# Two attention layers and two MLPs on one core: some row transposes move from TensorE to crossbar DMA

## The chip, the cores and the metric

The kernel runs on one core of a Trainium2 chip. The metric is the device time in microseconds (us). The core has TensorE (PE, with its weight loads shown as PEld), VectorE (DVE), ScalarE (ACT), GpSimd (POOL) and SyncE (SP). In this kernel SP issues all data movement by DMA, in the order of its queue: a DMA that waits for its data holds up every DMA behind it on SP. Eight DMA semaphores are used in turn, so a DMA also waits until the one eight places before it has landed.

## The reference

Four layers, each added to its own input: linear attention (A), MLP (B), A, B, on 2048 rows of 576 elements in bf16. Both kinds normalise rows first.

```python
def _layernorm(x, axis=-1, eps=1e-5):
    m = jnp.mean(x, axis=axis, keepdims=True)
    v = jnp.var(x, axis=axis, keepdims=True)
    return (x - m) / jnp.sqrt(v + eps)

# A: 32 heads of 18; phi(t) = where(t > 0, t + 1, exp(t)) + 1e-6
q, k, v = split_heads(x @ wqkv)              # wqkv 576 x 1728
kv  = sum over rows of phi(k) outer v        # per head
z   = sum over rows of phi(k)
o   = (phi(q) @ kv) / (phi(q) @ z + 1e-6)
return o @ wo                                # wo 576 x 576

# B: its own layernorm of an already normalised row; w1 576 x 4608, w2 4608 x 576
return gelu(layernorm(x) @ w1 + b1) @ w2 + b2
```

A and B use the same weights both times.

## The kernel before, in words

Rows are worked on in 16 tiles of 128 (t = 0 to 15). TensorE contracts over the partition axis, so normalised rows must be turned: column tile t of `yT` (128 partitions, KD = 5 blocks of 128 features, 2048 rows) holds the transposed rows of tile t, the last block holding 64 real features. Blocks of four tiles (512 rows, c = 0 to 3) are the unit of queries and of the MLP.

`LNPipe` carries each tile through normalisation. A tile is fed, and each `tick` moves it one stage on: statistics (on DVE by `bn_stats`, or on ACT), reciprocal root on POOL (line 433), a mean product (line 436), the norm itself (DVE for the first tiles of the first layer, POOL from tile 4 on, line 444; POOL for the first block of an MLP, line 466) and then the turning. `hold` leaves a tile alone for so many ticks. The recorded order within an engine is mostly the program's order; some instructions are tied to follow others by scheduling-only dependencies.

Rows are turned in one of two ways. With `evac` "act", PE transposes the five blocks against an identity into one PSUM bank (line 500) and ACT copies the bank into `yT` (line 505). With `evac` "dma", DVE turns 32 x 32 squares and a DMA through DRAM puts them in place; later MLP blocks and the second attention layer use this, and it does not change. The first way serves all 16 tiles of the first layer and, in both MLPs, the four tiles of the first block.

The first layer runs in rounds. For t from 4 to 15 a round is: the keys of tile t in two halves (`k_half`, line 653: five matmuls each, needing column tile t of `yT`), then `pre_a1`, which feeds a later tile, ticks the pipe and issues one piece of the weights that come later (`late_pieces`), then two steps of mask building on POOL, one group of queries (line 621) and the product of rows and keys (line 678). The function phi of a key half is either exp and identity on ACT with two steps on DVE (`phi_from_psum`) or exp on ACT and two steps on DVE of which one reads PSUM (`phi_by_dve`); the half chooses. The statistics of the tile that is fed follow the last phi on DVE.

The DMAs of the first layer's start and of the later weights are tied into one chain on SP (`chained`): input rows, wqkv, then the pieces of w1 (nine, three DMAs each), wo in their midst, then w2 (six pieces of 864 KB) with the bias b2 behind the second, then b1, then the residual rows `xo`.

After the keys come the small products of attention and then `wo_stage` for t from 0 to 15 (line 933): ten matmuls into a PSUM pair, a sum with the residual row on DVE (line 605), and a store of the new row to DRAM (`x_d`, line 612). Its tiles 0 to 3 are fed to the MLP's pipe. The MLP's first matmuls (line 1045) take all four tiles of the first block at once, and use the same PSUM pairs (`hp_ps`) that the sums of the last attention tiles must first have read. SP issues a residual load and a store for every tile there.

Of the kernel before, what the change touches and what calls it, by code (L numbers as in the profile page):

```python
# [15 lines left out]
P = 128  # L16
NT = S // P
KD = 5
# [17 lines left out]
def build(tc, A_x, A_wqkv, A_wo, B_w1, B_b1, B_w2, B_b2, out, dbg=None, n_layers=4):  # L36
    nc = tc.nc
    dbg = dbg or {}
    with ExitStack() as ctx:
# [90 lines left out]
        yT = const.tile([P, KD, S], BF16, name="yT")  # L130
# [4 lines left out]
        NV = 2  # L135
        v_ring = [const.tile([P, G, P], BF16, name=f"v_ring{i}") for i in range(NV)]
        AHEAD = 4
        turned = const.tile([P, D // 32, TPC, 32], BF16, name="turned")
        x_d = dpool.tile([NT, P, D], F32, name="x_d")
        yrow_d = dpool.tile([NCB, 4, TPC, 32, D], BF16, name="yrow_d")  # L140
# [112 lines left out]
        def bias_casts():  # L253
# [1 line left out]
            tc.add_manual_dep(cast.ins, pool_last["norm"], NOSYNC, reason="bias is not urgent")  # L255

        late_pieces = [(lambda i=i: piece_w1(i)) for i in range(4)] + [piece_wo] + \
                      [(lambda i=i: piece_w1(i)) for i in range(4, 9)] + [(lambda i=i: piece_w2(i)) for i in range(6)] + [piece_b1_dma]

        state = dict(wo=0, ycnt=0, vcnt=0, turns=0)  # L260
        pool_last = dict(norm=None)
# [85 lines left out]
        class LNPipe:  # L347
# [11 lines left out]
            def tick(self, transposes=1):  # L359
                land()  # L360
                for it in list(self.items):
                    st = it["stage"]
                    if st == 4 and it["evac"] != "dma":
                        if transposes == 0 or state["wo"] < it["tp_at"]:
                            continue
                        transposes -= 1
# [67 lines left out]
                    elif st == 2 and it["norm"] != "dve":  # L434
# [1 line left out]
                        nc.gpsimd.tensor_scalar(out=nmr[:], in0=it["mv"][:, 0:1], scalar1=1.0 if it["stats"] == "act" else -1.0,  # L436
                                                scalar2=it["rstd"][:, 0:1], op0=ALU.mult, op1=ALU.mult)
                        it["nmr"] = nmr
                    elif st in (2, 3) and it["kind"] == "A" and it["evac"] == "act":
                        xt, t = it["xt"], it["t"]  # L440
                        tail = first_tail(t)[:, 0:64]
                        if it["norm"] == "pool":
# [13 lines left out]
                    elif st in (2, 3):  # L456
                        if sum(other["stage"] == 4 for other in self.items) == NY:
                            continue
                        y = y_ring[state["ycnt"] % NY]
                        state["ycnt"] += 1  # L460
                        xt = it["xt"]
                        if it["norm"] == "act":
                            nc.scalar.activation(out=y[:, 0:D], in_=xt[:, 0:D], func=ACT.Identity,
                                                 scale=it["rstd"][:, 0:1], bias=it["nmr"][:, 0:1])
                        elif it["norm"] == "pool":
                            norm = nc.gpsimd.tensor_scalar(out=y[:, 0:D], in0=xt[:, 0:D], scalar1=it["rstd"][:, 0:1],
                                                           scalar2=it["nmr"][:, 0:1], op0=ALU.mult, op1=ALU.add)
                            pool_last["norm"] = norm.ins.name
                        else:
                            norm = nc.vector.tensor_scalar(out=y[:, 0:D], in0=xt[:, 0:D], scalar1=it["mv"][:, 0:1],  # L470
                                                           scalar2=it["rstd"][:, 0:1], op0=ALU.subtract, op1=ALU.mult)
                            if it["after"] == "phi":
                                tc.add_manual_dep(norm.ins, dve_last["phi"], NOSYNC, reason="keys go on first")
                            dve_last["norm"] = norm.ins.name
                        if it["kind"] == "B" and it["evac"] != "dma":
                            nc.gpsimd.tensor_copy(out=y[:, D:DPAD], in_=y[:, 4 * P:D])
                        if it["kind"] == "A" and it["evac"] == "dma":
                            c, j = divmod(it["t"], TPC)
                            nc.sync.dma_start(out=yrow_d[c, :, j], in_=y[:, 0:D])
                        it["y"] = y  # L480
                        it["stage"] = 4
                        continue
                    elif st == 4:
                        t = it["t"]
                        first_layer = it["kind"] == "A" and it["evac"] == "act"
                        y = it["xt"] if first_layer else it["y"]
                        if it["evac"] == "dma":
                            turn_rows(y, t, it["kind"])
                            self.items.remove(it)
                            continue  # L490
                        tp = ps_h.tile([P, 512], F32, name="tp", tag="h")
                        tp = tp[:, 0:DPAD // 2].bitcast(BF16).rearrange("p (k n) -> p k n", k=KD)
                        first = first_layer and t < 2
                        tp2 = tp
                        if first:
                            tp2 = ps_h.tile([P, 512], F32, name="tp2", tag="h")
                            tp2 = tp2[:, 0:DPAD // 2].bitcast(BF16).rearrange("p (k n) -> p k n", k=KD)
                        for k in range(KD):
                            block = first_tail(t, P) if first_layer and k == 4 else y[:, k * P:(k + 1) * P]
                            pe(nc.tensor.transpose(out=(tp if k < 3 else tp2)[:, k, :], in_=block, identity=ident[:]))  # L500
                        if first:
                            named(f"ca{t}", nc.scalar.copy(out=yT[:, 0:3, t * P:(t + 1) * P], in_=tp[:, 0:3, :]))  # L502
                            named(f"cd{t}", nc.vector.tensor_copy(out=yT[:, 3:KD, t * P:(t + 1) * P], in_=tp2[:, 3:KD, :]))
                        elif it["evac"] == "act":
                            turned_tile = nc.scalar.copy(out=yT[:, :, t * P:(t + 1) * P], in_=tp)
                            act_last["turned"] = turned_tile.ins.name
                            if first_layer and t < 5:
                                named(f"ca{t}", turned_tile)
                            elif act_last["exp"] is not None:
                                tc.add_manual_dep(turned_tile.ins, act_last["exp"], NOSYNC, reason="keys go on first")  # L510
                        else:
                            nc.vector.tensor_copy(out=yT[:, :, t * P:(t + 1) * P], in_=tp)
                        self.items.remove(it)
                        continue
# [100 lines left out]
        def layer_A(li, next_kind, pre_a1=None):  # L615
# [34 lines left out]
            def k_half(t, half, defer=False):  # L650
                kp = ps_h.tile([P, 512], F32, name="k_ps", tag="h")
                for k in range(KD):
                    pe(nc.tensor.matmul(kp[:, 0:HALF], lhsT=yT[:, k, t * P:(t + 1) * P],  # L653
                                        rhs=wqkv_sb[:, k, D + half * HALF: D + (half + 1) * HALF],
                                        start=(k == 0), stop=(k == KD - 1)))
                by_dve = half or li == 0 and t == 2

                def phi():
                    if (half, t // 2) not in self_k["pk"]:
                        self_k["pk"][(half, t // 2)] = blk.tile([P, D], BF16, name="pk", tag="blk")  # L660
                    pk = self_k["pk"][(half, t // 2)][:, (t % 2) * HALF:(t % 2 + 1) * HALF]
                    (phi_by_dve if by_dve else phi_from_psum)(kp[:, 0:HALF], pk, P, HALF,
                                                              tag=f"{t}{half}" if li == 0 and t < 4 else None)
                if defer:
                    return phi
                phi()
# [158 lines left out]
            if li == 0:  # L825
# [42 lines left out]
                    rows_by_keys(t, 0)  # L868
                for _ in range(2):
                    q_proj(*q_left.pop(0))  # L870
                masks(len(mask_steps))
            else:
                for t in range(6, NT - TPC):
# [63 lines left out]
            def wo_stage(t):  # L937
# [1 line left out]
                wp = wo_open[t][1]  # L939
                xn = residual(li, t, wp[:, :, 0:HALF])  # L940
                if xn is not None and next_kind == "B" and t < TPC:
                    lnp.feed(xn, t, "B", "pool", "act", hold=(2, 5, 6, 8)[t] if li > 0 else (2, 8, 8, 10)[t], tp_at=6 + 2 * t if li > 0 else (6, 10, 11, 14)[t],
                             **(dict(after="sum") if t in (0, 3 if li > 0 else 2) else dict(stats="act", after="rden")))

            for t in range(AHEAD if li == 0 else AHEAD + 2):
# [173 lines left out]
        def l0_norm_eng(t):  # L1119
            return "pool" if t > 3 else "dve"  # L1120

        def feed0(t, after=None):
            lnp.feed(x0_tiles.pop(t), t, "A", l0_norm_eng(t), "act", after=after)

        pe_chain.update(on=True, last=None)
        warm_pe(9)
# [7 lines left out]
        warm_pe(2)  # L1134

        def pre_a1_layer0(t):
            if t + 3 < NT:
                feed0(t + 3, after=dve_last["phi"])
            lnp.tick()
            if late_pieces:  # L1140
                late_pieces.pop(0)()
            if t == NT - 1:
                piece_b2_dma()
                while late_pieces:
                    late_pieces.pop(0)()

        lbs = {li: LayerB(li, kinds[li + 1] if li + 1 < n_layers else None)
               for li, kind in enumerate(kinds) if kind == "B"}
# [64 lines left out]
```

## Time and profile before

| what | value |
|---|---|
| median of 3 runs | 760.16 us (760.14 to 760.37) |
| span of the profiled execution, first to last instruction | 758.4 us |
| the runs' median less that span | 1.8 us |
| granted TensorE clock, mean | 1.000 |
| first layer's rounds, t = 4 to 15 | 17.9 to 56.8 us |
| first MLP's first matmul / second MLP's | 101.7 us / 473.6 us |
| first matmul with w2 | 136.8 us |
| PE transposes in all | 120 (24 tiles of five) |

The profile gives no time of its own for the profiled execution beside its span; what lies around the span is read as the difference to the runs. A line of the time order gives the start from the beginning of the span, the length, the engine, the source line, the operation, what it writes and reads, and how many instructions were merged. Matmuls overlap, so what a group adds is read from the start of one group to the start of the next. SP's own lines are issues: their length is the time that SP spent on issuing, and the landing is a separate figure (median of an issue of its line).

### The profile page before, as it was taken

The numbers are of one execution on the slowest core, as the hardware profiler recorded it, in microseconds if no ns is written. First come the engines' busy times: TensorE is split into PE (matmuls) and PEld (weight loads), VectorE is DVE, ScalarE is ACT, GpSimd is POOL, SyncE is SP. The second block draws the span as 40 slices with busy tenths as digits, with TensorE's granted clock in tenths as the row PEclk, the third lists the DMA queues.
The fourth block names the chain that finished last, engine by engine and source line by source line (L and its number), as shares of the span: only waits on it lengthen the run. The fifth ranks groups of instructions, "written<-read, shape, count | busy, mean of one in ns | idle before, by whom it ended". The sixth has DMA issues, their size and how long they took to land.

```text
span 758.4 us, 15817 instructions
## 1 busy us (share of the span) xinstructions
PE 753.2 (99%) x6595; PEld 487.4 (64%) x6595; DVE 272.0 (36%) x685; ACT 328.7 (43%) x733; POOL 116.6 (15%) x196
## 2 busy tenths in 40 slices
PE   9999999999999999999999999999999999999998
PEld 5776754774477457646777777457646754774476
DVE  8876862136033503401367577600230131000000
ACT  6887656205600650263057666660174036205600
POOL 4840231002000301200100005300020020001000
PEclk9999999999999999999999999999999999999999
DMA  8994573026312711320404047530240033011000
GB/s 236 267 313 74 178 262 82 17 64 189 83 39 83 181 51 48 109 69 17 131 24 116 24 136 255 185 82 16 88 115 7 16 127 82 9 33 55 1 9 24
DMA packets 80977, 73.90 MB, mean 97 GB/s; under 512 B 36874, under 2 KB 65546, under 8 KB 80906
## 3 DMA queue, kind: packets, MB, share of 16 engines
q1 hardware_dynamic: 80906, 72.90, 33.0%
q8 instruction: 51, 0.84, 0.5%
q14 instruction: 20, 0.16, 0.1%
HBM read 48.10 MB, written 24.77 MB: 96 GB/s over the span
## 4 chain that ended last, share of the span: by engine, by line
PE 97%; DVE 1%; ACT 0%; issue 0%; DVEq 0%
PE m_ps L1104 36%; PE h_ps L1045 21%; PE hp_ps L1045 16%; PE q_ps L621 6%; PE k_ps L653 5%; PE wo_ps L933 5%; PE k_ps L678 4%; PE m_half L1104 1%; PE tp L500 1%; PE warm_ps L217 1%; PE k_tail L678 1%; PE kv_ps L719 0%; PE den_ps L769 0%; PE rden_ps L810 0%; PE kvwo_half L737 0%
## 5 line engine op out<-in xcount | busy, mean ns | idle before, releaser
L1104 PE MATMUL m_ps<-w_sb,hT 128*128 128x288 bf16 x2232 | 274.8, 286 | 0.0
L1104 PEld LDWEIGHTS <-hT 128*128 128x128 bf16 x2304 | 224.3, 98 | 60.4 <-issue 3.4
L1045 PEld LDWEIGHTS <-w_sb 64*128 64x128 bf16 x2304 | 124.5, 94 | 136.4 <-issue 1.9
L1045 PE MATMUL hp_ps<-yT,w_sb 64*128 64x512 bf16 x1152 | 178.0, 376 | 0.0
L1045 PE MATMUL h_ps<-yT,w_sb 64*128 64x512 bf16 x1152 | 148.0, 376 | 0.0
L1050 ACT COPY relay_sb<-relay_sb 128x1 f32<-128x1 f32 x144 | 28.5, 198 | 260.4 <-PE h_ps L1045 217.6
L1041 ACT ACTIVATE hT<-h_ps,b1T 128x512 bf16<-128x512 f32 x144 | 91.0, 683 | 44.1 <-PE h_ps L1045 44.1
L433 POOL TENSOR_TENSOR ln_rstd<-ln_u,neg_half 128x1 f32<-128x1 f32 x61 | 35.2, 577 | 439.9 <-DVE ln_u L415 218.0
L1041 ACT ACTIVATE hT<-hp_ps,b1T 128x512 bf16<-128x512 f32 x144 | 91.1, 692 | 0.0
L605 DVE TENSOR_TENSOR xbf<-m_ps,xo 128x576 bf16<-128x576 f32 x15 | 11.4, 757 | 213.5 <-PE m_ps L1104 213.5
L605 DVE TENSOR_TENSOR xo<-m_ps,xo 128x576 f32<-128x576 f32 x16 | 12.1, 757 | 172.6 <-PE m_ps L1104 172.6
L588 POOL TENSOR_TENSOR xo<-xo,b_bc 128x576 f32<-128x576 f32 x32 | 40.9, 1283 | 97.3 <-DMA xo<-x_d 58.4
L1045 PE MATMUL h_ps<-yT,w_tail 64*128 64x512 bf16 x144 | 54.1, 376 | 0.0
L1045 PE MATMUL hp_ps<-yT,w_tail 64*128 64x512 bf16 x144 | 54.1, 376 | 0.0
L621 PE MATMUL q_ps<-yT,wqkv_sb 128*126 128x512 bf16 (+1 forms) x200 | 49.3, 379 | 0.1
L653 PE MATMUL k_ps<-wqkv_sb,yT 128*128 128x288 bf16 x320 | 44.6, 286 | 0.2
L933 PE MATMUL wo_ps<-kvwo,pq 126*128 126x288 bf16 (+1 forms) x320 | 43.4, 286 | 0.3
L1045 PEld LDWEIGHTS <-w_tail 64*128 64x128 bf16 x288 | 27.1, 94 | 17.1
L653 PEld LDWEIGHTS <-yT 128*128 128x128 bf16 x320 | 31.0, 98 | 8.9 <-ACT yT L502 0.6
L933 PEld LDWEIGHTS <-pq 126*128 126x128 bf16 (+1 forms) x320 | 30.3, 97 | 9.1 <-issue 0.8
L621 PEld LDWEIGHTS <-wqkv_sb 128*126 128x126 bf16 (+1 forms) x200 | 25.7, 131 | 11.7 <-issue 0.5
L554 ACT ACTIVATE phi_e<-q_ps 126x512 bf16<-126x512 f32 (+1 forms) x40 | 23.9, 597 | 18.4 <-PE q_ps L621 16.8
(138 smaller groups left out, 591.6 us busy)
## 6 DMA issues: line engine op xcount, KB each, us to landing
xo<-x_d SPq DMA_DIRECT2D x48, 288.0 KB, 3.5
x_d<-xo SPq DMA_DIRECT2D x32, 288.0 KB, 2.6
xl<-x_d SPq DMA_DIRECT2D x24, 288.0 KB, 4.2
y_d<-turned SPq DMA_DIRECT2D x40, 144.0 KB, 3.1
w_sb<-in_B_w_dram SPq DMA_DIRECT2D x6, 864.0 KB, 10.4
yT<-y_d SPq DMA_DIRECT2D x10, 512.0 KB, 4.2
w_sb<-in_B_w_dram SPq DMA_DIRECT2D x9, 512.0 KB, 5.9
x_d<-xn SPq DMA_DIRECT2D x16, 288.0 KB, 3.3
```

The lines of the kernel that those rows point to most:

```text
L433: nc.gpsimd.tensor_tensor(out=rstd[:], in0=it["u"][:], in1=neg_half[:], op=ALU.pow)
L554: exp = nc.scalar.activation(out=e_out, in_=ps_ap, func=ACT.Exp)
L588: nc.gpsimd.tensor_tensor(out=xo[:], in0=xo[:], in1=b2_bc[:], op=ALU.add)
L605: total = nc.vector.tensor_tensor(out=xn[:, cols].rearrange("p (h n) -> p h n", h=2), in0=halves, in1=xo[:, cols].rearrange("p (h n) -> p ...
L621: pe(nc.tensor.matmul(qp[0:GR[g], :], lhsT=wqkv_sb[:, k, GO[g]:GO[g] + GR[g]], rhs=yT[:, k, c * CA:(c + 1) * CA], start=(k == 0), stop=(k ...
L653: pe(nc.tensor.matmul(kp[:, 0:HALF], lhsT=yT[:, k, t * P:(t + 1) * P], rhs=wqkv_sb[:, k, D + half * HALF: D + (half + 1) * HALF], start=(k ...
L678: pe(nc.tensor.matmul(dst, lhsT=lhsT, rhs=pk, start=(t == 0), stop=(t == NT - 1)))
L933: pe(nc.tensor.matmul(wp[:, half, 0:HALF], lhsT=pq[(g, c)][0:GR[g], j * P:(j + 1) * P], rhs=kvwo[g][0:GR[g], half * HALF:(half + 1) * HALF ...
L1041: act_last["gelu"] = nc.scalar.activation(out=to, in_=ps, func=ACT.Gelu_apprx_tanh, bias=b1T[:, f:f + 1], scale=1.0).ins.name
L1045: mm = pe(nc.tensor.matmul(dst[n], lhsT=wt, rhs=mv, start=(seen[n] == 0), stop=(seen[n] == 8)))
L1050: relay = nc.scalar.copy(out=relay_sb[:, 1:2], in_=relay_sb[:, 0:1])
L1104: pe(nc.tensor.matmul(acc[half][:, 0:cols.stop - cols.start], lhsT=hT[f][:, j * P:(j + 1) * P], rhs=w2_sb[:, f, cols], start=(f == 0), sto ...
```

## The change

Crossbar DMA transposes, issued by SP straight from SBUF into `yT`, take the place of PE transposes with ACT copies for tiles 7 to 15 of the first layer and for the four tiles of the first block of both MLPs. In the first layer a tile takes two DMAs (its first four blocks from the row tile, the last from the ring that holds the row's last 64 features); in the MLP it takes one.

- The first layer's nine pairs are in the chain of SP, in between the weight pieces: two pieces of w1, tiles 7 and 8, a piece, tile 9, a piece, tile 10, wo, tile 11, and so on to tile 15, then the last piece.
- Statistics are fed four tiles ahead from tile 8 on (round 4 feeds tiles 7 and 8).
- The six pieces of w2 and b2 are issued behind the last round; b1 is issued in the last rounds' place of a piece.
- The keys' second half of tiles 7 to 15 goes through `phi_from_psum`.
- Tile 3 of the first MLP is held 9 ticks for 10; the places after which PE transposed (`tp_at`) fall away.

```diff
+        XB = 7
...
-                      [(lambda i=i: piece_w1(i)) for i in range(4, 9)] + [(lambda i=i: piece_w2(i)) for i in range(6)] + [piece_b1_dma]
+                      [(lambda i=i: piece_w1(i)) for i in range(4, 9)] + [piece_b1_dma]
+        w2_pieces = [(lambda i=i: piece_w2(i)) for i in range(6)]
...
-                    if st == 4 and it["evac"] != "dma":
+                    if st == 4 and it["evac"] not in ("dma", "xbar"):
...
+                        if it["evac"] == "xbar":
+                            if first_layer:
+                                chained(nc.sync.dma_start_transpose(out=yT[:, 0:KD - 1, t * P:(t + 1) * P], in_=y[:, 0:4 * P]))
+                                chained(nc.sync.dma_start_transpose(out=yT[:, KD - 1:KD, t * P:(t + 1) * P], in_=first_tail(t, P)))
+                            else:
+                                nc.sync.dma_start_transpose(out=yT[:, :, t * P:(t + 1) * P], in_=y[:])
+                            self.items.remove(it)
+                            continue
...
-                by_dve = half or li == 0 and t == 2
+                by_dve = half and (li > 0 or t < XB) or li == 0 and t == 2
...
+                piece_b2_dma()
+                for _ in range(6):
+                    w2_pieces.pop(0)()
                 masks(len(mask_steps))
...
-                    lnp.feed(xn, t, "B", "pool", "act", hold=(2, 5, 6, 8)[t] if li > 0 else (2, 8, 8, 10)[t], tp_at=6 + 2 * t if li > 0 else (6, 10, 11, 14)[t],
+                    lnp.feed(xn, t, "B", "pool", "xbar", hold=(2, 5, 6, 8)[t] if li > 0 else (2, 8, 8, 9)[t],
...
-            lnp.feed(x0_tiles.pop(t), t, "A", l0_norm_eng(t), "act", after=after)
+            lnp.feed(x0_tiles.pop(t), t, "A", l0_norm_eng(t), "act" if t < XB else "xbar", after=after)
...
-            if t + 3 < NT:
-                feed0(t + 3, after=dve_last["phi"])
+            for ahead in (3, 4) if t == 4 else (4,):
+                if t + ahead < NT:
+                    feed0(t + ahead, after=dve_last["phi"])
             lnp.tick()
-            if late_pieces:
+            if late_pieces and t < NT - 1:
                 late_pieces.pop(0)()
-            if t == NT - 1:
-                piece_b2_dma()
-                while late_pieces:
-                    late_pieces.pop(0)()
```

More of the change, by code (lines that the diff above doesn't have):

```diff
@@ L438, in tick @@
                         it["nmr"] = nmr
-                    elif st in (2, 3) and it["kind"] == "A" and it["evac"] == "act":
+                    elif st in (2, 3) and it["kind"] == "A" and it["evac"] in ("act", "xbar"):
                         xt, t = it["xt"], it["t"]
@@ L484, in tick @@
                         t = it["t"]
-                        first_layer = it["kind"] == "A" and it["evac"] == "act"
+                        first_layer = it["kind"] == "A" and it["evac"] in ("act", "xbar")
                         y = it["xt"] if first_layer else it["y"]
```

## The prediction

> **What bounds the kernel now.** I read the page's busy times first, then the chain, then the order in time of TensorE (PE), GpSimd (POOL) and SyncE's queue (SP) where the change sits.
>
> ```profile
> span 758.4 us, 15817 instructions
> PE 753.2 (99%) x6595; PEld 487.4 (64%) x6595; DVE 272.0 (36%) x685; ACT 328.7 (43%) x733; POOL 116.6 (15%) x196
> PE 97%; DVE 1%; ACT 0%; issue 0%; DVEq 0%
> PEclk9999999999999999999999999999999999999999
> ```
>
> PE is never short of work and always at full clock. So a matmul taken off PE shortens the span by its time, and a wait of PE lengthens it by its time. Nothing else counts. The span is 758.4 us; the median of the runs, 760.16, has 1.8 us more around it, which I leave unchanged, so the sum is taken from 760.16.
>
> PE in order of time in the first layer; start, length, what:
>
> ```profile
> 24.44 1.39 PE L653 MATMUL k_ps<-wqkv_sb,yT 128*128 128x288 bf16 x10
> 25.66 0.39 PE L500 MATMUL tp<-ident,x 128*128 128x128 bf16 x4
> 25.89 0.22 PE L500 MATMUL tp<-ident,v_ring 128*128 128x128 bf16 x1
> 26.02 1.24 PE L621 MATMUL q_ps<-yT,wqkv_sb 128*72 128x512 bf16 x5
> ...
> 27.70 1.39 PE L653 MATMUL k_ps<-wqkv_sb,yT 128*128 128x288 bf16 x10
> ...
> 53.89 1.39 PE L653 MATMUL k_ps<-wqkv_sb,yT 128*128 128x288 bf16 x10
> 55.11 1.24 PE L621 MATMUL q_ps<-yT,wqkv_sb 128*126 128x512 bf16 x5
> ```
>
> A round is 3.26 us (24.44 to 27.70). Five transposes hold PE from 25.66 to 26.02, 0.36 us; the last round has none. They turn tile 7, whose keys start at 27.70.
>
> POOL normalising tile 7, and SP's issues around it:
>
> ```profile
> 23.31 0.77 POOL L444 TENSOR_SCALAR x<-x,ln_rstd,ln_nmr 128x512 bf16<-128x512 bf16 x1
> 24.06 0.39 POOL L444 TENSOR_SCALAR v_ring<-x,ln_rstd,ln_nmr 128x64 bf16<-128x64 bf16 x1
> ```
> ```profile
> 19.14 0.60 SPq L231 DMA_DIRECT2D w_sb<-in_B_w_dram  x1
> 19.78 1.26 SPq L234 DMA_DIRECT2D w_tail<-in_B_w_dram  x2
> ...
> 24.95 0.63 SPq L226 DMA_DIRECT2D wo_sb<-in_A_wo_dram  x1
> 25.62 0.40 SPq L227 DMA_DIRECT2D wo_sb<-in_A_wo_dram  x1
> ```
>
> Tile 7 is normalised at 24.45, 3.25 us before its keys. Nothing on PE, ACT or POOL keeps SP from running ahead: one piece of the first MLP weight costs it 1.94 us (19.14 to 21.08), wo 1.03.
>
> **What goes.** Layer 1: 9 tiles at 0.355 us, 3.2 us of PE. The two MLP entries: 8 tiles, seven at 0.28 us (100.14 to 100.42) and one at 0.52 (466.40 to 466.92, an idle stretch within it), 2.45 us. Together **5.65 us**, all on the path. Seventeen ACT copies of 0.69 us go too, worth nothing, since PE is the bound.
>
> **What comes in layer 1.** The new key passes take 0.41 us on ACT (for 0.69) and 0.32 on DVE (for 0.46), nine each: both lighter, and between 27 and 55 us DVE is busy 23.5 of 28 us, ACT 22.9. I cost them at nothing; if DVE, the fuller, lost that cover, its 2.6 us a round would still be under PE's new 2.91 (3.26 less 0.355).
>
> Two crossbar DMAs per tile are new, and the trace has no such operation. Two prices are unknown. T, SP's time to issue the pair: the nearest rows are plain issues of 0.33 to 0.65 us (lowest T 0.66), and at the other end the bias load of 4608 two-byte elements at 2.31 us (T up to 2.96 with 0.65 for the tail). L, from an issue to its landing: 1.8 us (output rows) to 4.5 (slowest store of `turned`, median 3.1). I take T = 1.2 and L = 3.1, since that store, short runs out of SBUF, is nearest in kind.
>
> Tile 7 is first. Its keys are due at 27.70 - 0.36 = 27.34. Tile 8's statistics now stand between its own on DVE, two starts of 0.37 us, so its norm ends near 24.8 and 25.15. The second DMA goes at 24.8 + 0.6 = 25.4 and lands at 28.5. PE waits **1.2 us**. The DMA rings are near empty then, for SP now stops at these transposes from 21.1 on; the weight pieces stand behind them in its order.
>
> The tiles after: PE wants tile 15 at 27.34 + 8 x 2.91 = 50.6. SP starts on tile 8 at about 26.9 (its norm follows on POOL, 2.1 us after tile 7's), and has eight pairs, six weight pieces and wo: 26.9 + 8T + 6 x 1.94 + 1.03 = 39.6 + 8T, and the landing 2.5 us later. At T = 1.2 that is 51.7, which the first wait already covers. In that stretch the rings carry 6 x 0.59 + 0.66 + 8 x 0.164 = 5.5 MB in 23.6 us, 233 GB/s, against 289 at full share before (27 to 55 us). So a transpose often stands behind part of a weight piece, 0 to 2.0 us (0.59 MB at 289); I take half, **1.0 us**, paid once because the later tiles are then as late as PE. POOL needs 2.1 us per norm and 0.6 for masks, under 2.91; were it over, each tile would add the excess.
>
> The second MLP weight: its six pieces go out from about 52 instead of 40, and need 5.3 MB / 289 = 18 us, so the first residual rows land near 73, before the first sum at 80.3; its first matmul is at 136.8. The first MLP weight ends near 55, needed from 101.7. The bias vector lands before POOL's next norm at 83.9. All hidden by 7 us or more; a DMA stage 7 us slower than this would begin to cost.
>
> **What comes at the MLP entries.** The first block of the first MLP would start at 101.74 - 1.12 = 100.6. Tile 3's norm ended at 98.77; its square now stands on ACT ahead of a table load of 1.28 us and is held one tick less, so I put it at 97.2, and it lands at 100.3: no wait (1.3 us if the norm stays where it was). The next limit is a PSUM pair that the sum of tile 14 must free:
>
> ```profile
> 471.26 0.76 DVE L605 TENSOR_TENSOR xo<-wo_ps,xo 128x576 f32<-128x576 f32 x1 [0.81 <-PE wo_ps L933]
> 473.40 0.76 DVE L605 TENSOR_TENSOR xo<-wo_ps,xo 128x576 f32<-128x576 f32 x1 [1.39 <-DMA xo<-x_d]
> ```
>
> In the second MLP entry DVE waits for residual rows, whatever PE gains, and ends that sum at 474.16. The pair was wanted at 474.44 and is now wanted 1.1 us earlier: **0.85 us** given back; 0.1 at the first entry (sum ends at 101.61, wanted at 101.5). SP's order also puts the transposes of tiles 2 and 3 ahead of the last residual loads, up to 1.3 us if issuing them is dear; those loads wait for POOL anyway.
>
> **Sum.** -5.65 + 1.2 + 1.0 + 0.95 = -2.5; 760.16 - 2.5 = **757.6 us**.
>
> **Rivals.** *Slower: SP cannot issue fast enough.* With T larger, the wait before tile 15 is 39.6 + 8T + 2.5 - 50.6 = 8T - 8.5, with the 1.0 of the rings 8T - 7.5. The gain left, 5.65 - 0.95 = 4.7, is gone at **T = 1.5**. At T = 2 the time is 764.0, at 2.96 it is 771.6. For it: SP has in-order issue and weight pieces of 1.94 us in a round of 2.91, leaving 0.97. Against it: large plain DMAs of 512 runs cost only 0.4 to 0.6 us to issue. [...]
>
> *Better: wholly hidden.* With L = 1.8 tile 7's tail lands at 27.2, no wait: 760.16 - 4.7 = 755.5, or 754.5 if the residual loads come early too. For it: empty rings at 25 us; against it: only output stores land so fast.
>
> *Much slower: the crossbar holds the rings.* If each pair keeps them for r us, a round is r + 2.0 against 2.91; above r = 0.9 each of eight tiles adds the excess. At r = 4, 25 us of waiting, 780. The one row of element-wise movement, the bias load, took 12.7 us, but behind four pieces of the second weight. [...]
>
> **How the numbers follow.** Forecast (755.5 to 759.5): 0.46. Wholly hidden: 0.10. SP too slow: 0.34, its lower edge reaching 759 and most of it below 768. Rings held: 0.05. The change does nothing, gains given back exactly: 0.05. Taking 0.2% (1.5 us), about what a measurement tells from no change, the forecast gives 0.41 of faster, and hidden 0.10; the rest of the forecast, the 0.05 and the edge of the SP case give same 0.13; slower 0.36. The range 754.8 to 768 leaves out the held rings, the dearest issues, and a little below; the forecast's own range is 755.5 to 759.5.
>
> **What would show it.** PE: 85 transposes fewer; the keys' line then waits for a DMA on `yT`, 1 to 2 us near 27, little after. SP: the new issue lines' lengths give T, the landing L. A wait that comes back at every tile from 9 to 15 means T or the rings; one at 100 or 472 us means tile 3 was late; a DVE wait for residual rows near 473 with PE idle is the 0.85. It is wrong if T exceeds 1.5 us, or if L exceeds about 5.6 us (L - 1.9 for tile 7, plus 1.0, against 4.7).

## The result and the profile after

The changed kernel takes **778.83 us** (777.47 to 780.19) against 760.26 us for the kernel before: 1.0243 times as long, 95% interval 1.0228 to 1.0258. The forecast was 757.6 us, its range ended at 768, and the direction was wrong. The profiled execution has a span of 775.7 us, 17.3 more than before.

From the page of the changed kernel: the span, the busy times, the chain that ended last, and the granted clock.

```profile
span 775.7 us, 15669 instructions
PE 754.3 (97%) x6510; PEld 487.6 (63%) x6510; DVE 268.4 (35%) x685; ACT 321.4 (41%) x725; POOL 116.8 (15%) x196
PE 83%; DMA 2%; DVE 1%; ACT 0%; issue 0%; POOL 0%; SPq 0%; DVEq 0%; POOLq 0%
PEclk9999999999999999999999999999999999999999
```

PE has 85 matmuls fewer and is idle 21.4 us where it was 5.2; DMA has entered the chain. PE's busy time is no smaller although work was taken away, mostly because some of what is left ran at half clock (three windows of 3.41 us, some 1.7 us each), too briefly for the slices of the clock row to show it.

Where the 17.3 us came in, by the starts of the stages in the two traces (us):

| stretch | before | after | difference |
|---|---|---|---|
| start to the end of layer 1's key rounds | 59.06 | 68.49 | +9.43 |
| output products to the first MLP's first matmul | 23.78 | 27.35 | +3.57 |
| the same at the second MLP | 24.41 | 27.36 | +2.95 |
| second MLP's first matmul to PE's last | 281.90 | 283.33 | +1.43 |

The rest is unchanged. PE's waits in layer 1 (20 to 70 us; what waited for what: total, times, longest), and SP in the same stretch (start, length, what):

```profile
PE k_ps L663 <- DMA yT<-x: 4.5, 2, 2.6
PE k_ps L663 <- DMA yT<-v_ring: 2.2, 2, 1.7
PE k_ps L663 <- ACT phi_a L565: 0.5, 1, 0.5
PE k_tail L688 <- DVE pk L572: 0.4, 1, 0.4
```
```profile
45.25 1.23 SPq L495 DMA_TRANSPOSE yT<-x  x1
46.57 1.18 SPq L496 DMA_TRANSPOSE yT<-v_ring  x1
47.80 0.57 SPq L232 DMA_DIRECT2D w_sb<-in_B_w_dram  x1
48.43 1.26 SPq L235 DMA_DIRECT2D w_tail<-in_B_w_dram  x2
49.79 1.23 SPq L495 DMA_TRANSPOSE yT<-x  x1
```

SP hardly rests here: the gaps between these issues are 0.1 us or less, so it waits neither for a row nor for an earlier DMA. A pair of crossbar DMAs takes it 2.4 us of issue and some 2.6 with the gaps; with a weight piece of 1.9 a round of SP is 4.5 us (45.25 to 49.79), where a round of PE's own work is 2.91.

At the second MLP's entry (447 to 492 us), DVE's wait for residual rows before and then after (total, times, longest), and PE's wait for tile 3:

```profile
DVE xo L605 <- DMA xo<-x_d: 1.4, 1, 1.4
```
```profile
DVE xo L615 <- DMA xo<-x_d: 6.9, 4, 2.4
```
```profile
PE h_ps L1058 <- DMA yT<-y_ring: 1.7, 1, 1.7
```

At the first entry, tile 3's transpose on SP and the MLP's first matmul, which needs it:

```profile
110.71 1.29 SPq L498 DMA_TRANSPOSE yT<-y_ring  x1
```
```profile
114.75 1.04 PE L1058 MATMUL h_ps<-yT,w_sb 64*128 64x512 bf16 x8 [1.32 <-DMA yT<-y_ring]
```

### The profile page after: what moved, and what is told of

Its sections match the earlier page's. It is cut to its first block, busy times and chain, and to the rows that moved or that the text cites. A ratio compares the mean times of both kernels' runs of the same rounds, so it can differ in the third digit from the quotient of the medians.

```text
span 775.7 us, 15669 instructions
## 1 busy us (share of the span) xinstructions
PE 754.3 (97%) x6510; PEld 487.6 (63%) x6510; DVE 268.4 (35%) x685; ACT 321.4 (41%) x725; POOL 116.8 (15%) x196
## 4 chain that ended last, share of the span: by engine, by line
PE 83%; DMA 2%; DVE 1%; ACT 0%; issue 0%; POOL 0%; SPq 0%; DVEq 0%; POOLq 0%
PE m_ps L1117 35%; PE h_ps L1058 20%; PE hp_ps L1058 16%; PE q_ps L631 3%; PE k_ps L663 3%; PE k_ps L688 2%; PE wo_ps L946 1%; DMA yT<-y_ring 1%; PE m_half L1117 1%; DMA xo<-x_d 1%; DMA x_d<-xn 0%; DVE xn L615 0%; ACT turned L824 0%; PE k_tail L688 0%; DVE pq L830 0%
## 5 line engine op out<-in xcount | busy, mean ns | idle before, releaser
L1058 PEld LDWEIGHTS <-w_sb 64*128 64x128 bf16 x2304 | 128.4, 94 | 136.6 <-issue 6.5
L663 PE MATMUL k_ps<-wqkv_sb,yT 128*128 128x288 bf16 x320 | 47.6, 295 | 7.6 <-DMA yT<-x 4.5
L564 ACT ACTIVATE phi_e<-k_ps 128x288 bf16<-128x288 f32 x38 | 15.6, 410 | 48.3 <-PE k_ps L663 45.8
```

The lines of the kernel that those rows point to most:

```text
L564: exp = nc.scalar.activation(out=e_out, in_=ps_ap, func=ACT.Exp)
L1058: mm = pe(nc.tensor.matmul(dst[n], lhsT=wt, rhs=mv, start=(seen[n] == 0), stop=(seen[n] == 8)))
```

## The experiments

Theory: each crossbar DMA costs SP a fixed 1.2 us of issue, so in layer 1 the queue is the bound, and at the MLP entries the loads of residual rows stand behind the transposes. Rivals: the crossbar or the DMA rings are slow; the later second weight is itself the cause.

### The two halves of the change

Layer 1 alone: the feed at the MLP entries goes back.

```diff
-                    lnp.feed(xn, t, "B", "pool", "xbar", hold=(2, 5, 6, 8)[t] if li > 0 else (2, 8, 8, 9)[t],
+                    lnp.feed(xn, t, "B", "pool", "act", hold=(2, 5, 6, 8)[t] if li > 0 else (2, 8, 8, 10)[t], tp_at=6 + 2 * t if li > 0 else (6, 10, 11, 14)[t],
```

> The change in layer 1 and the later second weight are kept; the two MLP entries turn their rows on TensorE again. Theory 'SP's issue': each crossbar DMA holds SP's queue for about 1.2 us whatever its size, two of them and a weight piece make a round of 4.3 us against PE's 2.9, so layer 1 keeps its whole loss: it ends 9.4 us later than before, two clock halvings in it. The second MLP's entry goes back to 24.4 us (from 27.4), without its halving; the first MLP's entry keeps what the late second weight costs, 1 to 3 us. Sum 760.3 + 9.4 + 1 to 3 = 770.5 to 772.5. Rival 'the entries are only late because layer 1 is': the entries stay as in the changed kernel, 777.

769.82 us (1.0134, interval 1.012 to 1.0148), just under the range. Layer 1 ends 8.60 us late, and the first entry takes 24.88 us (+1.10). The second entry is back at 24.41. The 1.1 us are DVE's wait for the first residual pair, which the kernel before does not have at that sum:

```profile
DVE xn L615 <- DMA xo_pair<-in_A_x_dram: 1.2, 1, 1.2
```

The expected halvings did not come: after 17 us no matmul of this trace is as long as those at half clock. The changed kernel's key matmuls after its wait of 1.94 us, and here after the same wait:

```profile
45.22 2.54 PE L663 MATMUL k_ps<-wqkv_sb,yT 128*128 128x288 bf16 x10 [1.94 <-DMA yT<-x]
```
```profile
45.09 1.40 PE L663 MATMUL k_ps<-wqkv_sb,yT 128*128 128x288 bf16 x10 [1.94 <-DMA yT<-x]
```

The MLP entries alone: the kernel before with only that feed and its DMA.

```diff
+  if it["evac"] == "xbar":
+      nc.sync.dma_start_transpose(out=yT[:, :, t * P:(t + 1) * P], in_=y[:])
+      self.items.remove(it)
+      continue
```

> The kernel before with the crossbar only at the two MLP entries; layer 1 and the order of the second weight as before. Theory 'SP's issue': at the second entry the loads of residual rows stand behind three transposes of 1.3 us each on SP, so that stage takes 27.4 us instead of 24.4, and the half clock behind its wait adds 1.4: +4.4. At the first entry the residual pairs are early again (the second weight was issued long before), so only tile 3's landing is left, 1.3 us less the 1.1 us of transposes gone: +0.2 to +1. Sum 764.5 to 766. Rival 'the crossbar itself is slow at both entries': the first entry loses its 3.6 us too, 768.

769.0 us (1.0111, interval 1.0092 to 1.0129), above the range. The first entry takes 27.65 us although the second weight was issued early, so the late weight is not what costs there. In medians the halves add up: 9.6 and 8.8 above before, 18.6 together in the changed kernel. SP at the first entry, in the kernel before and then here:

```profile
82.04 1.72 SPq L612 DMA_DIRECT2D x_d<-xn  x2
83.88 0.38 SPq L575 DMA_DIRECT2D xo_pair<-in_A_x_dram  x1
```
```profile
82.49 1.72 SPq L616 DMA_DIRECT2D x_d<-xn  x2
86.55 1.34 SPq L492 DMA_TRANSPOSE yT<-y_ring  x1
88.44 0.41 SPq L579 DMA_DIRECT2D xo_pair<-in_A_x_dram  x1
```

SP stands at the transpose until tile 0 is normalised, from 84.2 to 86.55, and the residual pair behind it goes out 4.6 us later than before (4.1 when counted from the stage's own start, which is 0.45 us later here).

### Is it the number of DMAs, or their bytes?

One DMA per tile: the layer-1-only kernel without the one-block transposes (a memset at the start fills their place with zeros).

```diff
-  chained(nc.sync.dma_start_transpose(out=yT[:, KD - 1:KD, t * P:(t + 1) * P], in_=first_tail(t, P)))
```

> Layer 1 alone, with the four-block transposes of tiles 7 to 15 kept and the nine one-block transposes of their last 64 features left out (those rows of the transposed tile are zero, so the result lacks these features). A fifth of the bytes goes, half of the DMAs. Theory 'SP's issue': the pair's 2.4 us become 1.2, a round is 1.2 + 1.9 = 3.1 us against PE's 2.9; layer 1 ends 0 to 3 us earlier than before, not 9.4 later, that is 9 us or so under the layer-1-only kernel: about 761. Rival 'the crossbar or the rings are slow': four fifths of the movement are left, layer 1 keeps 7 us or more of its loss: 768 to 770.

759.71 us in a single run; layer 1 ends at 58.68, 9.0 us earlier than with two DMAs a tile, although four fifths of the bytes are left.

Three DMAs per tile: the same blocks, the wide one split.

```diff
-  chained(nc.sync.dma_start_transpose(out=yT[:, 0:KD - 1, t * P:(t + 1) * P], in_=y[:, 0:4 * P]))
+  for k in (0, 2):
+      chained(nc.sync.dma_start_transpose(out=yT[:, k:k + 2, t * P:(t + 1) * P], in_=y[:, k * P:(k + 2) * P]))
```

> Layer 1 alone; the four-block transpose of each tile 7 to 15 is split into two of two blocks, so each tile has three crossbar DMAs for the same 5 blocks and bytes. Theory 'a fixed issue per DMA': SP's time per tile goes from 2.4 to 3.55 us and a round with a weight piece from 4.4 to 5.5; seven to eight more rounds' worth of 1.17 us, so layer 1 ends 8 to 9 us later than with two DMAs (67.7 -> 76), and the late queue pushes the second weight's loads onto the residual pairs a little more: 778 to 781, against 769.8 with two and 759.7 with one. Rival 'bytes or blocks through the crossbar set the pace': same blocks, no change, 769 to 771.

781.05 us, also a single run. Layer 1 ends at 79.66, 12.0 us later than with two, more than the 8 to 9 expected: SP's eight rounds, 5.80 us for 4.54, give 10.1 of them, and three halvings of the clock lie in the same stretch. The first entry lost nothing more (24.03 us), against the expectation. SP's rows of the kernel with one, then of the one with three:

```profile
43.24 1.23 SPq L496 DMA_TRANSPOSE yT<-x  x1
44.52 0.58 SPq L233 DMA_DIRECT2D w_sb<-in_B_w_dram  x1
45.15 1.27 SPq L236 DMA_DIRECT2D w_tail<-in_B_w_dram  x2
46.52 1.23 SPq L496 DMA_TRANSPOSE yT<-x  x1
```
```profile
46.21 2.46 SPq L496 DMA_TRANSPOSE yT<-x  x2
48.77 1.18 SPq L497 DMA_TRANSPOSE yT<-v_ring  x1
49.99 0.59 SPq L232 DMA_DIRECT2D w_sb<-in_B_w_dram  x1
50.63 1.28 SPq L235 DMA_DIRECT2D w_tail<-in_B_w_dram  x2
52.01 2.50 SPq L496 DMA_TRANSPOSE yT<-x  x2
```

Two blocks cost about 1.23 us of issue, one block 1.18, four 1.23; a round is 3.28 us with one DMA and 5.80 with three. One, two and three DMAs a tile give 759.7, 769.8 and 781.1, differences of 10 us and more where the kernel with two spreads over 3: the number sets the time, and the rival of bytes falls.

### The queue freed

Two pieces of the first weight and wo go out before the transposes, the other seven behind them, the second weight in the first MLP's first groups; crossbar from tile 8 on, the MLP entries on PE.

```diff
-        XB = 7
+        XB = 8
-        late_pieces = [(lambda i=i: piece_w1(i)) for i in range(4)] + [piece_wo] + \
-                      [(lambda i=i: piece_w1(i)) for i in range(4, 9)] + [piece_b1_dma]
+        late_pieces = [(lambda i=i: piece_w1(i)) for i in range(2)] + [piece_wo]
+        rest_pieces = [(lambda i=i: piece_w1(i)) for i in range(2, 9)] + [piece_b1_dma, piece_b2_dma]
...
-                piece_b2_dma()
-                for _ in range(6):
-                    w2_pieces.pop(0)()
+                while rest_pieces:
+                    rest_pieces.pop(0)()
...
                         self.m1_group(c, g)
+                        if w2_pieces:
+                            w2_pieces.pop(0)()
...
+        while late_pieces:
+            late_pieces.pop(0)()
+
         def pre_a1_layer0(t):
...
-            if late_pieces and t < NT - 1:
-                late_pieces.pop(0)()
```

> Layer 1 alone with crossbar transposes from tile 8 on and an SP queue with nothing between them: two pieces of the first MLP weight and wo go out before, the other seven after the last transpose, the second weight during the first MLP's first groups. Theory 'SP's issue': a round on SP is 2.4 us against PE's 2.9, so no wait in layer 1, 8 x 0.355 = 2.8 us gained there, and no late residual rows: 757.5. Rival 'the crossbar or the rings are slow': PE still waits at most tiles, 763 or more.

758.68 us (0.998, interval 0.9971 to 0.9989): 0.2% faster than the kernel before. The same 5 blocks and two DMAs a tile as in the changed kernel, and no wait for a transpose is left on PE. This run also shows what a transposed tile takes of the rings. SP's last pairs, and then the stretch from 27 to 45 us, in which only transposes are in flight (columns: length, busy time of PE, PEld, DVE, ACT and POOL with instructions, clock, DMA share, GB/s):

```profile
41.81 1.21 SPq L495 DMA_TRANSPOSE yT<-x  x1
43.12 1.19 SPq L496 DMA_TRANSPOSE yT<-v_ring  x1
44.40 1.22 SPq L495 DMA_TRANSPOSE yT<-x  x1
45.71 1.18 SPq L496 DMA_TRANSPOSE yT<-v_ring  x1
46.98 1.22 SPq L495 DMA_TRANSPOSE yT<-x  x1
```
```profile
27.00:33.00 6.00, 5.93 (x42) 4.23 (x40) 5.57 (x19) 4.46 (x11) 5.52 (x15) 1.00 0.29 60
33.00:39.00 6.00, 5.88 (x40) 4.02 (x39) 5.44 (x20) 4.70 (x13) 5.44 (x13) 1.00 0.29 55
39.00:45.00 6.00, 5.89 (x41) 4.11 (x40) 5.37 (x20) 4.82 (x12) 5.25 (x13) 1.00 0.27 55
```

A pair every 2.59 us, back to back, stays under PE's 2.91. A share of 0.28 over a round of 3.1 us is 0.87 us of the rings per tile.

Layer 1 gained 1.74 us, though, where eight tiles less should give 2.84. PE's rounds from tile 7 to 12 take 2.94 to 3.19 us, 1.1 us in all over 2.92, and the two after take 2.92. DVE is busy 5.4 of 6 us in them, and its instructions make up about half of the chain of waits from 27 to 47 us. POOL is as busy (5.3 to 5.5 us), but is not in that chain.

### What paces the shortened rounds

In the kernel with the freed queue, the lighter pass on DVE from tile 5 on (below), from tile 7 (XB - 1) and from tile 6 (XB - 2):

```diff
-                by_dve = half and (li > 0 or t < XB)
+                by_dve = half and (li > 0 or t < XB - 3)
```

> The kernel with the freed queue (758.7), with the second half of the keys of tiles 5 to 7 moved from VectorE's long pass (0.46 us) to the pass shared with ScalarE (0.31). Theory 'VectorE paces layer 1's shortened rounds' (they take 3.05 to 3.19 us from tile 8 to 12 where TensorE's own work is 2.91, and VectorE starts into them behind): VectorE saves 0.45 us by tile 8, layer 1 ends 0.3 to 0.5 us earlier: 758.2 to 758.4. Rival 'ScalarE paces them' (three key passes more on it): no gain or a loss of as much, 758.7 to 759.2.

> The freed queue (758.7) with the lighter VectorE pass from tile 7 on. Theory 'both engines pace these rounds': ScalarE has one extra pass of 0.41 us in its last round with a copy of a transposed tile, which it can still take, and VectorE 0.15 us less: rounds 8 to 12 lose 0.2 to 0.5 us less than with the pass from tile 8: 758.2 to 758.6. Rival 'only the number of statistics counts': no change, 758.7.

> The same from tile 6 on. Theory 'both engines pace these rounds': VectorE 0.3 us lighter by tile 8, ScalarE two passes (0.8 us) heavier in rounds that are 3.26 us long: between the gain from tile 7 and the wait of 1.0 us that came from tile 5 on: 758.2 to 758.9. Rival 'only the number of statistics counts': no change, 758.7.

758.93, 758.70 and 758.80 us (intervals 0.9974 to 0.9991, 0.9970 to 0.9988, 0.9972 to 0.9990): no gain in any; the times fit the rivals' forecasts, and the rounds tell more than the times. With the pass from tile 5 on, the rounds from tile 8 do fall to 2.92 us, but the rounds of tiles 6 and 7 grow (3.41 and 4.07 us), with one wait for keys that come late from DVE behind ACT:

```profile
PE k_tail L688 <- DVE pk L572: 1.0, 1, 1.0
```

The keys of tiles 11 and 12 with the freed queue, and then with the lighter pass from tile 5 on:

```profile
40.08 1.39 PE L663 MATMUL k_ps<-wqkv_sb,yT 128*128 128x288 bf16 x10
43.27 1.39 PE L663 MATMUL k_ps<-wqkv_sb,yT 128*128 128x288 bf16 x10
```
```profile
40.76 1.39 PE L663 MATMUL k_ps<-wqkv_sb,yT 128*128 128x288 bf16 x10
43.68 1.39 PE L663 MATMUL k_ps<-wqkv_sb,yT 128*128 128x288 bf16 x10
```

From tile 8 on both kernels hold the same instructions, and one keeps rounds of 2.92 us with them while the other's reach 3.19. So no engine has too much work for a round of 2.92, DVE and POOL included. What the freed queue loses looks like a lag that is paid once: one kernel pays it at tiles 6 and 7, the other bit by bit up to tile 12. With the pass from tile 7 or 6 on, the rounds from tile 8 to 12 add up to 15.5 us as without it, so that a lighter pass as such speeds them is not shown. That the lag is DVE's is argued from its half of the chain, and where it arises stays open.

The statistics four tiles ahead, and both halves of the keys alike, were also tried in the kernel before, where PE still turns every tile.

```diff
-            if t + 3 < NT:
-                feed0(t + 3, after=dve_last["phi"])
+            for ahead in (3, 4) if t == 4 else (4,) if t > 4 else (3,):
+                if t + ahead < NT:
+                    feed0(t + ahead, after=dve_last["phi"])
...
-                by_dve = half or li == 0 and t == 2
+                by_dve = half and (li > 0 or t < 7) or li == 0 and t == 2
```

> The kernel before with the statistics four tiles ahead from tile 8 on and the key passes of tiles 7 to 15 alike on both halves, while TensorE still turns every tile: rounds of 3.26 us. Theory 'the added VectorE and ScalarE work hides while a round is 3.26 us': no change, 759.9 to 760.7. Rival 'the extra statistics make PE wait by themselves': the 1.0 us that rounds 7 to 12 lose with the freed queue shows here too, 761.2.

760.48 us (1.000, interval 0.9991 to 1.0009): the added work is free in rounds of 3.26 us. That this work is what costs 1.1 us when PE's rounds shrink is not shown.

### The MLP entries: order on SP, or landing?

The entries-only kernel with the DMA issued by ACT.

```diff
-  nc.sync.dma_start_transpose(out=yT[:, :, t * P:(t + 1) * P], in_=y[:])
+  nc.scalar.dma_start_transpose(out=yT[:, :, t * P:(t + 1) * P], in_=y[:])
```

> The two MLP entries alone, their transposes issued from ScalarE's queue instead of SP's; layer 1 as before. Theory 'residual loads stand behind the transposes on SP': SP's loads are as early as before, DVE's waits for them go back to those of the kernel before; what stays is the landing of tile 3 (0.7 to 2.5 us of PE per entry) and ScalarE's own 1.3 us per issue: 762 to 765, against 769.0 from SP. Rival 'the transposes slow the other transfers in the rings': the loads land as late as from SP, 768 to 770.

774.01 us (1.0185, interval 1.0158 to 1.0211): slower still, so both forecasts missed. The mechanism can be seen all the same. DVE's waits for residual rows at the second entry, with SP issuing:

```profile
DVE xo L609 <- DMA xo<-x_d: 6.1, 4, 2.0
```

With ACT issuing, no such wait is left at either entry, and at the first one the pairs go out at 83.86 and 87.37 us, as in the kernel before (83.88 and 87.39), with a transpose issued between them: it is not in the rings that the transposes hold the loads up, but by their place in SP's queue. (At the second entry DVE is itself held up 8 us by ACT, which would hide some lateness.) But now ACT is the queue that stands (first entry):

```profile
83.63 0.38 ACT L778 ACTIVATE rden<-den_ps 128x256 bf16<-128x256 f32 x1
86.08 1.31 ACTq L492 DMA_TRANSPOSE yT<-y_ring  x1
87.44 2.05 ACT L818 CAST turned<-rden_ps 126x512 bf16<-126x512 f32 x4 [3.42 <-issue]
```

The copies behind the transpose started after 3.4 us of standing, and PE waited 1.9 us for them from 86.2 us on. Before the first MLP PE was idle for 3.62 us, and a window at half clock followed (mean granted clock of the run 0.996). The profile names no releaser for that wait; tile 3's transpose, which the matmul needs, went out last, at 102.10, and the matmul started at 107.76.

Tile 3 alone back on PE, the others by SP:

```diff
-                    lnp.feed(xn, t, "B", "pool", "xbar", hold=(2, 5, 6, 8)[t] if li > 0 else (2, 8, 8, 9)[t],
+                    lnp.feed(xn, t, "B", "pool", "xbar" if t < 3 else "act", hold=(2, 5, 6, 8)[t] if li > 0 else (2, 8, 8, 10)[t], tp_at=6 + 2 * t if li > 0 else (6, 10, 11, 14)[t],
```

> The two MLP entries alone from SP's queue, but tile 3 of each block is turned on TensorE as before; tiles 0 to 2 by the crossbar. Theory 'two causes: loads behind the transposes, and tile 3's landing': the wait of PE before the first block of each MLP goes (2.5 and 0.7 us, and the half clock behind them, 1.7 each), the waits for residual rows stay: 763 to 765. Rival 'the landing of tile 3 is the whole loss': back to 760 or less. Rival 'the order on SP is the whole loss': no change, 768 to 770.

764.62 us (1.0052, interval 1.0035 to 1.0068): half the loss goes with tile 3's transposes and the half clock behind them (none here), half stays. Two things go at once here, the wait for tile 3's landing and one transpose less in SP's queue at each entry, and their shares are not told apart. In what stays, PE is idle four times for over 1 us for the rows' sums, 1.45, 1.26, 1.37 and 1.11 us, 5.2 in all.

### The later second weight alone

```diff
-                      [(lambda i=i: piece_w1(i)) for i in range(4, 9)] + [(lambda i=i: piece_w2(i)) for i in range(6)] + [piece_b1_dma]
+                      [(lambda i=i: piece_w1(i)) for i in range(4, 9)] + [piece_b1_dma]
+        w2_pieces = [(lambda i=i: piece_w2(i)) for i in range(6)]
...
                     q_proj(*q_left.pop(0))
+                piece_b2_dma()
+                for _ in range(6):
+                    w2_pieces.pop(0)()
...
-            if late_pieces:
+            if late_pieces and t < NT - 1:
                 late_pieces.pop(0)()
-            if t == NT - 1:
-                piece_b2_dma()
-                while late_pieces:
-                    late_pieces.pop(0)()
```

> The kernel before with one part of the change: the second MLP weight's pieces (and the bias) issued after the last key round, not in it. No crossbar anywhere. Theory 'the later weight costs only behind a late SP queue': SP has issued all first-weight pieces by about 44 us, the weight goes out from 55 or so, the residual pairs land by 75, before the first sum at 80.3: no change, 759.9 to 760.6. Rival 'the later weight itself makes the residual pairs late', as in the changed kernel and in the layer-1-only kernel: +1.1, 761.3.

760.48 us (1.0001, interval 0.9992 to 1.0011). Later in the program is hardly later in time when SP runs ahead of the engines. Its rows here, and those of the changed kernel:

```profile
43.75 10.88 SPq L239 DMA_DIRECT2D w_sb<-in_B_w_dram  x6
54.67 9.19 SPq L576 DMA_DIRECT2D xo_pair<-in_A_x_dram  x3
```
```profile
69.55 10.97 SPq L240 DMA_DIRECT2D w_sb<-in_B_w_dram  x6
80.56 4.00 SPq L585 DMA_DIRECT2D xo_pair<-in_A_x_dram  x3
```

The first residual pair went out at 53.5 in the kernel before, at 54.7 here, and at 80.6 where the crossbar pairs hold SP.

## Why the prediction was wrong, point by point

- **T, SP's time for a pair: the step that failed.** Taken as 1.2 us, it is 2.4, and 2.6 with the gaps. I took the price from the nearest kind of transfer, a store of short runs; the issue of a crossbar DMA cost SP 1.16 to 1.37 us in the changed kernel with one, four or five blocks (medians 1.17, 1.23 and 1.30, some 0.03 us for a block more) and about 1.23 with two (2.46 to 2.50 for two issues with three DMAs a tile), and a tile has two DMAs (one issue from ACT took 1.97 us). The formula around it held: 8T - 8.5 at 2.6 is a wait of 12.3 us before tile 15, which puts its keys at 62.9; they started at 63.32, and at 62.18 with layer 1 alone. Less 3.2 us of transposes that is a loss of 9.1, against 9.43 measured and 8.60 with layer 1 alone. The break-even of T = 1.5 was passed far, and the rival "SP cannot issue fast enough" is what happened. Layer 1 alone gives 769.82 us; the rest up to 778.83 came at the entries.
- **Tile 7's first wait**, put at 1.2 us, did not come: its first transpose went out at 24.11, landed at 26.64, and its keys ran at 27.32 without a wait. The waits for transposes came at tiles 9, 10, 11 and 14 instead.
- **L, issue to landing**: taken as 3.1; of the changed kernel's landings that the trace holds in layer 1, one took 2.5 us with quiet rings (24.11 to 26.64), the others, among weight pieces, 2.8, 4.1 and 4.5. Right in size.
- **The rings**: 1.0 us allowed, and "the crossbar holds the rings" at 0.05. With 0.87 us a tile they are just under the 0.9 that was named as the bound. In the changed kernel their share from 28 to 69 us was 0.68, against 1.03 from 28 to 59 before: they waited for SP. Four blocks landed 2.53 us after their issue, and five take 0.87 us of the rings, far below the r = 4 of that rival.
- **The MLP entries**: costed at -1.0 and -0.5 us, they are +3.57 and +2.95, and 1.43 more in the second MLP. Two steps failed. "Those loads wait for POOL anyway" dismissed the transposes ahead of residual loads; DVE's wait for them at the second entry grew from 1.4 to 6.9 us, and with the transposes off SP it is gone. "No wait" for tile 3 took its landing at 3.1 us; it was issued at 110.71 and PE started at 114.75, after a wait of 1.32. Its norm, put at 97.2, ended at 110.2, or 100.8 without the 9.43 us that layer 1 lost, so the transpose also went out late. Nor was it counted that SP also stands at a transpose whose row isn't normalised yet, with the loads behind (84.2 to 86.55 us with the entries alone).
- **The second weight, "hidden by 7 us or more"**: right alone, wrong where SP is late, since the cover was SP's own lead. Behind the late queue it cost 1.1 us with layer 1 alone.
- **DVE, ACT and POOL "at nothing"**: right while PE's round is 3.26, and the work fits a round of 2.92 too; but on the way there 1.1 of 2.84 us stayed away in the kernel with the freed queue, as a lag that the prediction has no term for.
- **The clock**: "always at full" was taken over to the changed kernel; three halvings in its trace, one in the second MLP worth 1.43 us. In layer 1 they cost little, for SP was the bound: 9.43 us with two of them, 8.60 without.
- **What went, 5.65 us of PE work**: right in layer 1, where a round falls from 3.26 to 2.92; the best run, with the entries on PE, had 1.5 us of it.

## What to carry to other kernels

Price a DMA by what its issue holds up: the issuing engine pays for each crossbar transpose (1.2 to 1.3 us here, for one block or five), and pays again, standing, for every row that isn't ready (some 2.3 us for tile 0 with the entries alone), with all that is behind it in the same queue. Before moving work from a bounding engine to a queue, add up that queue's round against the new round of the bound, and check that slack elsewhere ("hidden by 7 us") isn't the lead of that very queue. Where no row of the trace has the price, split or halve the number of such instructions first: it tells a price per instruction from a price per byte in two runs.

## What the runs showed of the hardware beyond that

In these traces the granted clock falls to half for 3.41 us at a time, on a grid of windows of that length (in the changed kernel from 45.30, 58.95 and 489.03 us, 4 and 126 windows apart), and an idle time shorter than a window was enough (1.94 us before the first of these). The window before such a fall and the halved one behind it, in the changed kernel's layer 1:

```profile
41.89:45.30 3.41, 1.47 (x10) 0.82 (x9) 2.64 (x9) 1.53 (x4) 1.82 (x5) 1.00 1.10 218
45.30:48.71 3.41, 3.41 (x13) 1.98 (x14) 0.91 (x4) 1.42 (x4) 1.36 (x3) 0.50 0.76 200
```

The traces of the changed kernel and of the runs with entries alone (from SP and from ACT) and three DMAs a tile hold ten such falls after 20 us. Laid on the grid that the falls give, PE was idle 1.68 to 3.00 us of the 3.41 in each window before them; of the other windows with over 1 us of idle time, thirteen, all had 1.52 or less but one, with 1.74. So, as an estimate from these windows, the bound lies at about half of one (1.68 us was enough once; 1.74 was not, in the changed kernel from 35.06 us). The same wait of 1.94 us halved the clock in one run and not in another; that the grid cut it in two there is a guess, for that trace holds no clock record. Where PE is the bound, a fall cost 1.7 us: in the kernel with the entries alone (mean granted clock 0.66 from 105 to 110 us), the first MLP from its first matmul to the first with w2 took 36.76 us against 35.07.
